# Routing scratch moved from a PSUM bank to SBUF, first group's ranks half a chunk later

## The chip, the cores and the metric

The kernel runs on one core of one Trainium2 chip. The metric is device time in microseconds (us) of one execution. The core has a TensorE (PE, with its weight loads as PEld), a VectorE (DVE), a ScalarE (ACT), a GpSimd (POOL) and a SyncE (SP), which work through their own instruction lists in order and wait for each other by semaphores. Operands lie in SBUF or in PSUM, whose banks hold 128 x 512 float32 each and take the results of matmuls.

## What is computed

The reference chains three layers, all in float32:

```python
# linear attention with decay: batch 4, heads 8, 768 steps, head_dim 48
for t in range(S):
    state = alpha[:, :, t, :, None] * state + np.einsum('bhd,bhe->bhde', k[:, :, t], v[:, :, t])
    y[:, :, t] = np.einsum('bhd,bhde->bhe', q[:, :, t], state)
# mixture of 8 experts, 3072 tokens, width 384, hidden 1024
logits = x @ w_gate
noise_scale = np.log1p(np.exp(x @ w_noise))
noisy_logits = logits + noise_scale * noise
top2 = np.argpartition(-noisy_logits, 2, axis=1)[:, :2]
...
h = np.maximum(x[mask] @ w1[e], 0.0)
out[mask] += top2_w[mask, k, None] * (h @ w2[e])
# dense gated layer, hidden 1536
return (a * b @ w_out).astype(np.float32)
```

## The kernel before

**Attention.** 24 chunks `i` of 128 tokens (6 for each of 4 batch entries) pass through the loop at L756 to L783. For each chunk TensorE does, in this order: the transposes of the next chunk's keys (`t_unit`, L643), the transposes of the previous chunk's result (`gx_unit`, L724), the part of the result that comes from the carried state (`inter`, L667), the scores of the next chunk (`sc_unit`, L651), the part of the result from inside the chunk (`intra`, L675), the gate's matmuls for the previous chunk (`gm_unit`, L736) and the state's update (`u_unit`, L702). VectorE masks the scores (L656) and makes the running products of the decay for a chunk three ahead (`prep`: scans L621 and L625, L620, L624). GpSimd multiplies keys and queries by them (L623, L626, L629), and with ScalarE it prepares expert weights beside this (`w_tick`: L110 on ScalarE, L111 on GpSimd). The state goes over VectorE's L717 or L714, GpSimd's L718 and ScalarE's L691.

**Routing beside it.** Four times in a chunk the loop calls `tick()`, which advances every generator in the list `side` to its next `yield`. So the order of the work is written out by hand: a `yield` more moves what follows by a quarter of a chunk. `gm_unit` appends a `routing` at the end of each set of chunks in `SUBS = (0, 5, 10, 14, 19, 24)`. It runs `choose`, which finds the two experts of every token of a set: ScalarE lists the logits out of the gate's bank 6 (L258, L259), ScalarE and GpSimd work out the noise's scale (L262 to L280), VectorE adds it (L284), and two passes of L290, L293, L294, L297, L298 find the largest and, after L302 has masked it, the second largest. Behind the last set of a group (`GROUPS = (14, 10)`, so sets 0 to 2 and sets 3 and 4) follow `route` and `lists`. `route` counts the tokens of each expert by a scan (L330), four matmuls into bank 5 (L337 to L343) that give the ranks, twelve small VectorE operations (L349 to L370), two wide comparisons (L376), 14 small matmuls (L384) and the sums with `lacc` (L388, L390), from which come the indices of expert 0's gathers (L479). `lists` does the same for the other seven experts (L412 to L449).

**Where the scratch lies.** `scratch` gives the small tiles of `choose` and `route` columns of bank 5 from 136 on, by way of `place`, unless the set is the last one, which has tiles in SBUF named `s_...`. The factor of the first scan, `d0[0]`, lies in bank 5 as well. `spot` gives the results of the matmuls their columns: the early ones in bank 5 (0 for ranks, 128 for lists), the others in bank 6 (`UG`) or a free bank.

**Behind it.** Eight experts of up and down products, each as three matmuls (`prod3`, L801 to L803), then the dense layer (L1117 to L1122). Of the first `up_unit`s some are given banks 5 and 6 among others.

Of the kernel before, what the change touches and what calls it, by code (L numbers as in the profile page):

```python
# [7 lines left out]
F32 = mybir.dt.float32  # L8
# [15 lines left out]
E = 8  # L24
# [13 lines left out]
GROUPS = (14, 10)  # L38
SUBS = (0, 5, 10, 14, 19, 24)
LAG = 3  # L40
WL = (E - 1) * NJ
# [16 lines left out]
def moe_kernel(ctx: ExitStack, tc, qka, afirst, v, wgn, noise, w1, w2, w3, out):  # L58
# [4 lines left out]
    def tl(pool, shape, dt, tag, **kw):  # L63
        uid[0] += 1
        return pool.tile(shape, dt, tag=tag, name=f"{tag}_{uid[0]}", **kw)
# [4 lines left out]
    def bank(i):  # L70
        return tl(psum, [128, 512], F32, f"bank{i}")
# [80 lines left out]
    rt = tc.alloc_tile_pool(name="rt", bufs=1, side="right")  # L152
# [3 lines left out]
    def trbank():  # L156
        trn[0] += 1
        return bank(trn[0] % 2)
# [13 lines left out]
    oh = [tl(rt, [128, NT, E], F32, f"oh{k}") for k in range(2)]  # L172
    oas = [tl(rt, [128, E, n + 1], F32, f"oa{n}") for n in GROUPS]
    B5 = bank(5)
    c0 = [136]

    def place(shape, name=None, dt=F32):

        if name:
            return tl(rt, [128, *shape], dt, name)  # L180
        n = 1
        for x in shape:
            n *= x
        a = B5[:, c0[0]:c0[0] + n]
        c0[0] += n
        a = a if dt == F32 else a.bitcast(dt)
        return a if len(shape) == 1 else a.rearrange("p (a b) -> p a b", a=shape[0])

    d0 = [place((E, GROUPS[0] + 1)), place((E, GROUPS[1] + 1), "d0")]
    SMALL = {}  # L190

    def scratch(name, shape, late, dt=F32):
        if late:
            return tl(rt, [128, *shape], dt, "s_" + name)
        if name not in SMALL:
            SMALL[name] = place(shape, None, dt)
        return SMALL[name]

    def iota(t, pattern, base=0, channel=0):
        nc.gpsimd.iota(t, pattern=pattern, base=base, channel_multiplier=channel,  # L200
# [18 lines left out]
    groups, i0 = [], 0  # L219
# [9 lines left out]
    def spot(kind, n, early=False):  # L229

        if early:
            return B5[:, (0, 128)[kind]:(0, 128)[kind] + n]
        c = (NP * 48, 288)[kind]
        return small[0][:, c:c + n] if small else trbank()[:, :n]

    def choose(s):
# [10 lines left out]
        def scr(name, *shape):  # L247
            return scratch(name, (5, *shape), last)[:, :n]
# [62 lines left out]
    def route(g):  # L311

        tiles = groups[g]
        n = len(tiles)
        i0 = tiles[0]
        sh = [128, n, E]
        last = g == len(groups) - 1
# [5 lines left out]
        def scr(name, dt=F32):  # L323
            return scratch(name, (n,), last, dt)
# [5 lines left out]
        nc.vector.tensor_tensor_scan(xc.rearrange("p e j -> p (e j)"), d0[g].rearrange("p e j -> p (e j)"),  # L330
                                     oa.rearrange("p e j -> p (e j)"), 0.0, op0=ALU.mult, op1=ALU.add)
        carry[0] = xc[:, :, n]
        for _ in range(LAG - 1):
            yield
        pb = spot(0, n * E + E + 1, not last)
        pc = pb[:, n * E:n * E + E]
        nc.tensor.matmul(pc, ones, xc[:, :, n], start=True, stop=True)  # L337
# [42 lines left out]
        for _ in range(LAG - 1):  # L380
            yield
        pl = spot(1, NJ, not last)
        for j in range(n):
            nc.tensor.matmul(pl, ats[j // m][:, j % m], bt[:, j], start=j == 0, stop=j == n - 1)  # L384
# [21 lines left out]
    def lists(g):  # L406

        i0, i1 = groups[g][0], groups[g][-1] + 1
        n = i1 - i0
        pi, ki, pf, kf = (tl(rt, [128, max(GROUPS), 2], dt, x)[:, :n]  # L410
                          for x, dt in (("ei", I32), ("ri", I32), ("rf", F32), ("e1", F32)))
        nc.vector.tensor_scalar(pi, slot[:, i0:i1], 127, None, op0=ALU.bitwise_and)  # L412
        nc.vector.tensor_scalar(ki, slot[:, i0:i1], 7, None, op0=ALU.logical_shift_right)
        nc.vector.tensor_copy(pf, pi)
        nc.vector.tensor_copy(kf, ki)
        sets = [(a, b) for a, b in zip(SUBS, SUBS[1:]) if i0 <= a < i1]
        hot = {}

        def make(s):
            j0, j1 = s  # L420
            m = j1 - j0
            at, eq, bt = (tl(rt, [128, HOT, 2, w_], F16, x, bufs=2)[:, :m]
                          for x, w_ in (("at", 128), ("eqk", WL), ("bt", WL)))
            for out_, src, val in ((at, lane, pf), (eq, keys[:, NJ:], kf)):
                w_ = src.shape[-1]
                nc.vector.tensor_tensor(out_.rearrange("p a k w -> p (a k) w"),
                                        src[:, None, :].to_broadcast([128, 2 * m, w_]),
                                        val[:, j0 - i0:j1 - i0].rearrange("p a k -> p (a k)")[:, :, None]
                                        .to_broadcast([128, 2 * m, w_]), op=ALU.is_equal)
                yield  # L430
            for k in range(2):
                nc.vector.tensor_tensor(bt[:, :, k], eq[:, :, k],
                                        token[:, j0:j1, None].to_broadcast([128, m, WL]), op=ALU.mult)
            hot[s] = m, at, bt

        yield from make(sets[0])
        for s, after in zip(sets, sets[1:] + [None]):
            if after:
                yield from make(after)
            else:  # L440
                for _ in range(LAG - 1):
                    yield
            m, at, bt = hot.pop(s)
            pl = spot(1, WL)
            for j in range(m):
                for k in range(2):
                    nc.tensor.matmul(pl, at[:, j, k], bt[:, j, k], start=j + k == 0, stop=j == m - 1 and k == 1)
            yield
            nc.vector.tensor_tensor((idx if s[1] == NT else lacc)[:, NJ:], pl, lacc[:, NJ:], op=ALU.add)  # L449
        yield  # L450
# [99 lines left out]
    def routing(s):  # L550
        yield from choose(s)
        g = group_of[SUBS[s]][0]
        if SUBS[s + 1] == groups[g][-1] + 1:
            yield from route(g)
            yield from lists(g)
        if SUBS[s + 1] == NT:
            for q in range(NJ):
                gather(1, q)
                yield
            yield from weights()  # L560
# [521 lines left out]
    for f in range(NF1):  # L1082
# [5 lines left out]
        if f in (4, 5, 7):  # L1088
            i = min(f - 4, 2)
# [69 lines left out]
    for u in range(NB * NF2):  # L1159
        blk, f = divmod(u, NF2)  # L1160
# [127 lines left out]
```

## Time and profile before

| what | us |
|---|---|
| median of 3 runs (1049.27 to 1050.80) | 1050.78 |
| the profiled execution, its own time | 1048.68 |
| its span in the trace | 1046.9 |
| TensorE busy | 1004.8 (96%) |
| VectorE busy | 563.0 (54%) |
| GpSimd busy | 411.9 (39%) |
| ScalarE busy | 384.9 (37%) |

The span runs from the first to the last recorded instruction; 1.8 us of the execution lie outside it. A row of a timeline gives the start, the duration, the engine, the line of the kernel, the operation, the tiles written and read, and, in brackets, how long the engine was idle before it and whose work ended that. `bank` stands for a PSUM tile, every other name for an SBUF tile or DRAM. Shares of busy time are averages over stages: attention with the routing takes the first 150 us, and from then on TensorE is busy almost without a gap.

### The profile page before, as it was taken

Reading aid. Unit: us, or ns where it says so; the run is one execution under the profiler, and the core shown is the slowest. Engines: PE = TensorE matmul, PEld = TensorE weight load, DVE = VectorE, ACT = ScalarE, POOL = GpSimd, SP = SyncE. Lnnn points to the kernel's source line nnn. Section 1 sums busy time; section 2 is a strip of 40 time slices with the busy share of each in tenths; the row PEclk is TensorE's granted clock in tenths of the full one; section 3 lists DMA queues with packets and bytes.
Section 4 is the critical chain, followed back from the end, with each engine's and each line's share of the span. In section 5 each row is a group of like instructions: output and inputs, shape, how many; then the busy total and the mean of one; then the engine's idle time right before and its main releaser. Section 6 shows DMA issues by size and latency. Waiting matters only on the chain.

```text
span 1046.9 us, 17559 instructions
## 1 busy us (share of the span) xinstructions
PE 1004.8 (96%) x6686; PEld 929.2 (89%) x6686; DVE 563.0 (54%) x987; ACT 384.9 (37%) x831; POOL 411.9 (39%) x443
## 2 busy tenths in 40 slices
PE   7998789999999999999999799999999999999996
PEld 5887679999999999999989688888888888888886
DVE  8999667576767776777646354242233232333221
ACT  2555331454454454545434243222222222222221
POOL 5688432575667686868644244020020020000000
PEclk9999779999999999999999899999999999999999
DMA  8787111669686869687845635131040140020000
GB/s 327 262 300 266 34 54 38 184 182 257 181 235 199 228 204 267 208 226 239 214 138 161 168 99 144 52 91 31 32 115 6 46 106 1 31 61 1 31 1 33
DMA packets 121491, 142.71 MB, mean 136 GB/s; under 512 B 68400, under 2 KB 105392, under 8 KB 121392
## 3 DMA queue, kind: packets, MB, share of 16 engines
q1 hardware_dynamic: 114864, 121.71, 38.7%
q0 software_dynamic: 6528, 19.67, 6.6%
q8 instruction: 64, 1.05, 0.4%
q14 instruction: 35, 0.29, 0.1%
HBM read 102.21 MB, written 39.12 MB: 135 GB/s over the span
## 4 chain that ended last, share of the span: by engine, by line
PE 86%; DVE 7%; DMA 2%; POOL 2%; issue 2%; ACT 1%; SPq 0%; POOLq 0%; ACTq 0%; DVEq 0%
PE bank L801 26%; PE bank L802 26%; PE bank L803 26%; PE bank L651 2%; PE bank L667 1%; DVE pm L656 1%; DVE D L621 1%; DVE A L625 1%; PE bank L675 1%; PE bank L643 1%; PE bank L702 1%; PE bank L611 1%; DMA wd<-w 0%; DMA raw<-xt 0%; PE bank L487 0%
## 5 line engine op out<-in xcount | busy, mean ns | idle before, releaser
L1119 DVE TENSOR_TENSOR p<-bank,a 128x512 f32<-128x512 f32 x72 | 49.8, 691 | 253.5 <-PE bank L803 253.5
L111 POOL TENSOR_TENSOR W<-wst,W 128x384 fp32r<-128x384 f32 x136 | 146.1, 1085 | 91.0 <-ACT W L110 83.1
L801 PE MATMUL bank<-X,W 128*128 128x416 f32 (+4 forms) x474 | 168.7, 356 | 2.9 <-DVE HB L846 2.5
L801 PE MATMUL bank<-HB,W 128*128 128x416 f32 (+4 forms) x474 | 167.2, 353 | 0.9 <-DVE o L874 0.9
L802 PE MATMUL bank<-X,W 128*128 128x416 f32 (+3 forms) x474 | 167.9, 354 | 0.0
L803 PE MATMUL bank<-X,W 128*128 128x416 f32 (+3 forms) x474 | 167.7, 354 | 0.0
L803 PE MATMUL bank<-HB,W 128*128 128x416 f32 (+3 forms) x474 | 166.5, 351 | 0.0
L802 PE MATMUL bank<-HB,W 128*128 128x416 f32 (+3 forms) x474 | 166.5, 351 | 0.0
L975 POOL DMA_INDIRECT row<-y,row x48 | 47.1, 981 | 203.9 <-DVE row L983 170.4
L1117 ACT ACTIVATE a<-bank 128x512 f32<-128x512 f32 x72 | 43.0, 597 | 167.0 <-PE bank L803 167.0
L845 ACT ACTIVATE HB<-bank 128x416 fp32r<-128x416 f32 (+2 forms) x128 | 65.7, 516 | 105.2 <-PE bank L803 105.1
L1121 ACT ACTIVATE HB<-p 128x512 fp32r<-128x512 f32 x72 | 45.5, 632 | 157.1 <-DVE p L1119 157.1
L801 PEld LDWEIGHTS bank<-X,W 128*128 128x128 f32 x474 | 89.8, 189 | 7.4 <-DVE HB L846 3.2
L846 DVE SCALAR_TENSOR_TENSOR HB<-bank,HB 128x416 fp32r<-128x416 f32 (+2 forms) x128 | 72.7, 582 | 41.0 <-ACT HB L845 40.9
L801 PEld LDWEIGHTS bank<-HB,W 128*128 128x128 f32 x474 | 89.1, 188 | 4.9 <-DVE o L874 1.2
L803 PEld LDWEIGHTS bank<-X,W 128*128 128x128 f32 x474 | 89.7, 189 | 4.1
L802 PEld LDWEIGHTS bank<-X,W 128*128 128x128 f32 x474 | 89.7, 189 | 3.6
L803 PEld LDWEIGHTS bank<-HB,W 128*128 128x128 f32 x474 | 89.0, 188 | 4.0
L802 PEld LDWEIGHTS bank<-HB,W 128*128 128x128 f32 x474 | 89.0, 188 | 3.7
L1122 DVE TENSOR_TENSOR HB<-p,HB 128x512 fp32r<-128x512 f32 x72 | 49.8, 692 | 50.2 <-ACT HB L1121 50.2
L110 ACT ACTIVATE W<-wst 128x384 fp32r<-128x384 f32 x144 | 72.1, 515 | 8.8 <-DMA wst<-w 7.2
L479 POOL DMA_INDIRECT row<-xd,idx x56 | 58.6, 1046 | 39.9 <-DVE idx L388 23.2
(240 smaller groups left out, 1954.3 us busy)
## 6 DMA issues: line engine op xcount, KB each, us to landing
wst<-w SPq DMA_DIRECT2D x128, 192.0 KB, 4.3
ring<-qka SPq DMA_DIRECT2D x22, 768.0 KB, 6.5
wd<-w SPq DMA_DIRECT2D x36, 384.0 KB, 4.5
xt<-tb SPq DMA_DIRECT2D x12, 768.0 KB, 4.6
raw<-xt SPq DMA_DIRECT2D x48, 192.0 KB, 4.4
y<-o SPq DMA_DIRECT2D x56, 156.0 KB, 2.8
w3f<-u SPq DMA_DIRECT2D x36, 192.0 KB, 2.8
wst<-w3f SPq DMA_DIRECT2D x36, 192.0 KB, 3.0
```

Of the source, the lines that this page charges most:

```text
L110: nc.scalar.activation(h, raw, AF.Copy)
L111: eng.tensor_tensor(l, raw, h.bitcast(F32), op=ALU.subtract)
L479: nc.gpsimd.indirect_dma_start(out=t[:m], out_offset=None, in_=xd[:SPLIT * 128] if a else xd, in_offset=bass.IndirectOffsetOnAxis(ap=ix, a ...
L801: nc.tensor.matmul(ps[:, :m], ah, bh[:, :m], start=first, stop=False)
L802: nc.tensor.matmul(ps[:, :n], ah, bl[:, :n], start=False, stop=False)
L803: nc.tensor.matmul(ps[:, :n], al, bh[:, :n], start=False, stop=last)
L845: nc.scalar.activation(Hh[:, f, s], pu[:, :n], AF.Relu)
L846: nc.vector.scalar_tensor_tensor(Hl[:, f, s], pu[:, :n], 0.0, Hh[:, f, s].bitcast(F32), op0=ALU.max, op1=ALU.subtract)
L975: nc.gpsimd.indirect_dma_start(out=t, out_offset=None, in_=src, in_offset=bass.IndirectOffsetOnAxis(ap=row[:, i, k:k + 1], axis=0))
L1119: nc.vector.tensor_tensor(p, ps[1], a, op=ALU.mult)
L1121: nc.scalar.activation(h, p, AF.Copy)
L1122: nc.vector.tensor_tensor(l, p, h.bitcast(F32), op=ALU.subtract)
```

## The change

Three things change. The small tiles of `choose` and `route` and the factor of the first scan are SBUF tiles for all sets, named `s_...0` for the earlier sets and `s_...1` for the last. The early results of matmuls get columns 0 and 256 of bank 5, and the sums of the first group's `lists` are early too, so they go to bank 5 instead of bank 6. The first group's rank matmuls stand `LAG + 1` = 4 ticks behind the scan instead of `LAG - 1` = 2, half a chunk.

```diff
     B5 = bank(5)
-    c0 = [136]
-
-    def place(shape, name=None, dt=F32):
...
-    d0 = [place((E, GROUPS[0] + 1)), place((E, GROUPS[1] + 1), "d0")]
-    SMALL = {}
+    d0 = [tl(rt, [128, E, n + 1], F32, f"d0{i}") for i, n in enumerate(GROUPS)]
 
     def scratch(name, shape, late, dt=F32):
-        if late:
-            return tl(rt, [128, *shape], dt, "s_" + name)
-        if name not in SMALL:
-            SMALL[name] = place(shape, None, dt)
-        return SMALL[name]
+        return tl(rt, [128, *shape], dt, f"s_{name}{int(late)}")
...
         if early:
-            return B5[:, (0, 128)[kind]:(0, 128)[kind] + n]
+            return B5[:, 256 * kind:256 * kind + n]
...
         carry[0] = xc[:, :, n]
-        for _ in range(LAG - 1):
+        for _ in range(LAG - 1 if last else LAG + 1):
             yield
...
         n = i1 - i0
+        waiting = g == len(groups) - 1
...
-            pl = spot(1, WL)
+            pl = spot(1, WL, not waiting)
```

The changed file is 18 or 19 lines shorter ahead of the attention loop, so L667 there is L649, L702 is L684, L337 is L318 and L293 is L274.

On TensorE the ranks of the first group stood between the transposes of chunk 19 and its `inter`. `xc` is the scan's result and `bank_30` is bank 5. Before:

```order
L702 MATMUL bank_32_121<-v_1335,kn_1799 48x48 x8
L643 MATMUL bank_371_1877<-ident_71,ring_37_132 128x128 x4
L724 MATMUL bank_373_1884<-ident_71,x_1849 128x128 x3
L337 MATMUL bank_30_119<-xc_367_1859,ones_77 128x8
L340 MATMUL bank_30_119<-xc_367_1859,ones_77 128x1
L342 MATMUL bank_30_119<-oa_28_117,before_75 128x112
L343 MATMUL bank_30_119<-xc_367_1859,ones_77 128x112
L667 MATMUL bank_375_1894<-Sbd_45_151,ring_36_131 128x96 x4
```

Now they stand behind the gate's matmuls and ahead of the state's update (L684):

```order
L657 MATMUL bank_391_1906<-v_1344,pm_379_1838 64x48 x2
L718 MATMUL bank_33_122<-wgn_104,gx_1904 64x16 x6
L318 MATMUL bank_30_119<-xc_383_1875,ones_77 128x8
L321 MATMUL bank_30_119<-xc_383_1875,ones_77 128x1
L323 MATMUL bank_30_119<-oa_28_117,before_75 128x112
L324 MATMUL bank_30_119<-xc_383_1875,ones_77 128x112
L684 MATMUL bank_33_122<-v_1543,kn_1898 48x48 x8
```

So the chunk's own `inter`, scores and `intra` no longer have the scan ahead of them.

On VectorE one pass of `choose` (the second one of a set) stays where it is, behind the scan L625 and around the L717, and changes its operands. `r_m` and `r_mk` are SBUF tiles in both. Before:

```order
L625 SCALAR_TENSOR_TENSOR A_1371<-ring_38_133,bank_33_128 128x512
L302 SCALAR_TENSOR_TENSOR bank_30_119<-oh_26_115,bank_30_119 128x40
L290 TENSOR_REDUCE r_m_281_1381<-bank_30_119 128x5
L293 TENSOR_TENSOR bank_30_119<-bank_30_119,r_m_281_1381 128x40
L294 TENSOR_TENSOR bank_30_119<-bank_30_119,prio_107 128x40
L717 TENSOR_TENSOR ss_1421<-bank_32_121,sc_1324 128x192
L297 TENSOR_REDUCE r_mk_282_1382<-bank_30_119 128x5
L298 TENSOR_TENSOR oh_27_116<-bank_30_119,r_mk_282_1382 128x40
```

Now:

```order
L607 SCALAR_TENSOR_TENSOR A_1380<-ring_40_135,bank_34_129 128x512
L283 SCALAR_TENSOR_TENSOR s_nl_290_1389<-oh_26_115,s_nl_271_1319 128x40
L271 TENSOR_REDUCE r_m_292_1392<-s_nl_290_1389 128x5
L274 TENSOR_TENSOR s_eq_291_1391<-s_nl_290_1389,r_m_292_1392 128x40
L275 TENSOR_TENSOR s_eq_291_1391<-s_eq_291_1391,prio_107 128x40
L699 TENSOR_TENSOR ss_1432<-bank_33_122,sc_1333 128x192
L278 TENSOR_REDUCE r_mk_293_1393<-s_eq_291_1391 128x5
L279 TENSOR_TENSOR oh_27_116<-s_eq_291_1391,r_mk_293_1393 128x40
```

The order is the same; the operations that had one SBUF input and one in the bank have two in SBUF.

Further on VectorE the two wide comparisons L376, which stood directly behind the small route operations and one L717, now stand behind the next chunk's masks and `prep` (L602 to L607):

```order
L351 TENSOR_TENSOR bt_2025<-eqk_2024,s_val_414_1992 128x98
L638 TENSOR_TENSOR pm_427_2046<-bank_425_2036,causal_73 128x512
L638 TENSOR_TENSOR pm_428_2048<-bank_426_2037,causal_73 128x512
L602 MEMSET bank_34_129 128x3
L603 SCALAR_TENSOR_TENSOR D_44_147<-ring_41_136,bank_34_129 128x511
L606 RECIPROCAL bank_34_129<-D_44_147 128x4
L607 SCALAR_TENSOR_TENSOR A_2050<-ring_41_136,bank_34_129 128x512
L357 TENSOR_TENSOR at_2059<-lane_109,s_pf_412_1990 128x896
L357 TENSOR_TENSOR at_2089<-lane_109,s_pf_412_1990 128x896
```

They moved with the ranks, by half a chunk; the 14 matmuls that read `at` (L384 before) moved on TensorE to a place between a chunk's scores and its `intra`.

## Rows read from the trace of the kernel before

**Rows 1.** The page, part 4: shares of the chain by engine and line.

```profile
PE 86%; DVE 7%; DMA 2%; POOL 2%; issue 2%; ACT 1%; SPq 0%; POOLq 0%; ACTq 0%; DVEq 0%
PE bank L801 26%; PE bank L802 26%; PE bank L803 26%; PE bank L651 2%; PE bank L667 1%; DVE pm L656 1%; DVE D L621 1%; DVE A L625 1%; PE bank L675 1%; PE bank L643 1%; PE bank L702 1%; PE bank L611 1%; DMA wd<-w 0%; DMA raw<-xt 0%; PE bank L487 0%
```

**Rows 2.** The chain, 50 to 112 us: start, duration, engine, tile, line.

```profile
63.89 1.29 DVE pm L656 x2
...
77.09 0.11 DVE bank L284
...
83.99 0.56 DVE pm L656
...
94.41 0.69 DVE pm L656
...
108.55 0.31 DVE xc L330
```

**Rows 3.** The timeline, 100 to 126 us, TensorE and VectorE.

```profile
108.90 0.39 PE L337 MATMUL bank<-xc,ones 128*128 128x8 f32 x2 [2.76 <-DVE xc L330]
...
113.27 1.29 DVE L656 TENSOR_TENSOR pm<-bank,causal 128x512 f32<-128x512 f32 x2 [4.17 <-PE bank L651]
...
119.47 0.26 DVE L370 TENSOR_TENSOR bt<-eqk,bank 128x98 f16<-128x98 f16 x1
...
120.00 0.88 PE L702 MATMUL bank<-v,kn 128*48 128x48 f32 x16 [4.30 <-ACT bank L259]
...
121.03 0.36 DVE L717 TENSOR_TENSOR ss<-bank,sc 128x192 f32<-128x192 f32 x1 [1.30 <-PE bank L702]
...
125.64 0.69 DVE L656 TENSOR_TENSOR pm<-bank,causal 128x512 f32<-128x512 f32 x1 [2.27 <-PE bank L651]
```

**Rows 4.** Busy time by window (us, PE, PEld, DVE, ACT, POOL), granted clock.

```profile
112.00:114.00 2.00, 2.00 (x28) 1.77 (x28) 0.73 (x2) 0.00 (x0) 0.00 (x0) 0.50 0.03 8
```

**Rows 5.** The timeline, 147 to 161 us, TensorE.

```profile
158.03 0.33 PE L801 MATMUL bank<-X,W 128*128 128x384 f32 x1
```

**Rows 6.** Instructions of line L942 (ns min/median/max), and timelines around 105, 143 and 252 us.

```profile
L942 DVE TENSOR_SCALAR u<-wd x36: 339/348/1470, 194.1 to 532.7; 128x384 int32<-128x384 int32 x36
...
105.60 0.26 POOL L306 TENSOR_TENSOR oa<-oh,oh 128x32 f32<-128x32 f32 x1
...
143.47 0.66 DVE L426 TENSOR_TENSOR eqk<-keys,e 128x490 f16<-128x490 f16 x1
...
143.63 0.63 POOL L306 TENSOR_TENSOR oa<-oh,oh 128x40 f32<-128x40 f32 x1 [3.39 <-DVE oh L298]
...
144.05 0.23 DVE L307 TENSOR_TENSOR dm<-r_m,r_m 128x5 f32<-128x5 f32 x1
...
251.10 2.62 POOL L111 TENSOR_TENSOR W<-wst,W 128x384 fp32r<-128x384 f32 x2
...
252.76 1.17 DVE L942 TENSOR_SCALAR u<-wd 128x384 int32<-128x384 int32 x1
```

**Rows 7.** The timeline, 74 to 106 us, VectorE and GpSimd.

```profile
76.84 1.28 POOL L623 TENSOR_TENSOR ring<-ring,D 128x512 f32<-128x512 f32 x1
...
77.01 0.18 DVE L284 TENSOR_TENSOR bank<-r_sp,bank 128x40 f32<-128x40 f32 x1
...
78.08 1.27 POOL L626 TENSOR_TENSOR ring<-ring,A 128x512 f32<-128x512 f32 x1
...
79.46 0.51 POOL L718 TENSOR_TENSOR sc<-ss,aend 128x192 f32<-128x192 f32 x1
...
82.42 0.18 DVE L302 SCALAR_TENSOR_TENSOR bank<-oh,bank 128x40 f32<-128x40 f32 x1
...
82.65 1.27 POOL L626 TENSOR_TENSOR ring<-ring,A 128x512 f32<-128x512 f32 x1 [0.22 <-DVE bank L302]
...
82.87 0.21 DVE L293 TENSOR_TENSOR bank<-bank,r_m 128x40 f32<-128x40 f32 x1
```

**Rows 8.** Instructions of line L293: ns min/median/max, first and last start.

```profile
L293 DVE TENSOR_TENSOR bank<-bank,r_m x8: 198/199/208, 53.3 to 140.9; 128x40 f32<-128x40 f32 x6, 128x32 f32<-128x32 f32 x2
L293 DVE TENSOR_TENSOR s_eq<-s_nl,r_m x2: 200/200/201, 156.0 to 157.4; 128x40 f32<-128x40 f32 x2
```

More of the change, by code (lines that the diff above doesn't have):

```diff
@@ L174, in moe_kernel @@
     B5 = bank(5)
-    c0 = [136]
-    def place(shape, name=None, dt=F32):
[L179 to L187, printed above, removed]
-    d0 = [place((E, GROUPS[0] + 1)), place((E, GROUPS[1] + 1), "d0")]
-    SMALL = {}
-    def scratch(name, shape, late, dt=F32):
-        if late:
-            return tl(rt, [128, *shape], dt, "s_" + name)
-        if name not in SMALL:
-            SMALL[name] = place(shape, None, dt)
-        return SMALL[name]
+    d0 = [tl(rt, [128, E, n + 1], F32, f"d0{i}") for i, n in enumerate(GROUPS)]
+    def scratch(name, shape, late, dt=F32):
+        return tl(rt, [128, *shape], dt, f"s_{name}{int(late)}")
     def iota(t, pattern, base=0, channel=0):
```

## The prediction, made before the changed kernel ran

> **What bounds the kernel now.** I read the chain of waits first. Over the whole span it is TensorE by 86% [rows 1], and 78% of the span are the three products L801 to L803, which the change leaves as they are. So only the time ahead of them, attention with the routing beside it, can change, and what matters there is when these products may begin.
>
> Inside that stretch I read the chain again, with a window [rows 2]. TensorE is not the chain everywhere. VectorE carries it at 63.9 us, from before 77.09 to 83.99 and from 94.41 to 108.86. Those stretches hold the small VectorE operations of the second and third `choose`: L284, L290, L293, L294, L297, L298, then L302 and once more L290 to L298. The step at 83.99 us is the L656 that stands behind the whole pass. So a VectorE operation that gets longer there moves the end one for one.
>
> Then the timeline around the first group's ranks [rows 3]. L337 waits 2.76 us for the scan L330 and holds the whole of chunk 19's TensorE work behind it, since TensorE works in order. 11 us later L702 waits 4.30 us for ScalarE's L259, which lists the logits into bank 5 and had to wait for L370, the last of the twelve small route operations that use bank 5. VectorE pays too: its L656 stands idle for 4.17 us, its L717 for 1.30 us and the next L656 for 2.27 us, each time for TensorE. [...]
>
> **Part one, the ranks half a chunk later and the bank freed: a gain.** The four rank matmuls move behind chunk 19's scores, intra and gate matmuls. L330 is done at 108.86 us [rows 2] and they come after that, so the 2.76 us go. With the scratch in SBUF, L259 no longer has to wait for L370, so the 4.30 us go as well. What is late next is VectorE: without the idle time it is busy from there to the lists of the first group, and it holds the bound. Its end moves by the idle time it had for TensorE, 4.17 + 1.30 + 2.27 = 7.74 us. I take 0.7 us off for a new wait: the 14 matmuls L384 now stand one unit earlier on TensorE, behind two L376 on VectorE that stand a prep later. That makes **-7 us**. Bounds: 0, if the wait only changes its name, and -10, if the tail of the lists does not bind. In between lies the place where the lists' sums bind: the last of them shares bank 5 with the expert product that starts at 158.03 us [rows 5], which therefore waits for the sum.
>
> **Part two, the scratch in SBUF: a loss.** Each operation of `choose` reads and writes bank 5 now. Then it would read two SBUF tiles, and GpSimd is reading SBUF at the same time. What the trace says of such a pair [rows 6]: the scalar operation L942 takes 348 ns in the median. The one at 252.76 us stood beside GpSimd's L111 until 253.72 and took 1.17 us, ending 0.21 us behind it. Smaller ones do the same at 143.47 us: VectorE's L426, two SBUF inputs, ran until 144.13, and GpSimd's L306 took 0.63 us instead of the 0.26 of 105.60 us and ended at 144.26. VectorE's L307, 128x5 with two SBUF inputs, then took 0.23 us and ended at 144.28. So whoever comes second stands until the other is done, whatever its size. The bank forms stand beside GpSimd untouched: L284 at 77.01 us inside L623, and L293 at 82.87 us inside L626, both took about 0.2 us [rows 7].
>
> Now the price of one `choose`, with these rows. First pass: L284 would come at 77.01 us, while L623 runs until 78.12: +1.1 us. L293 then meets L626, which has started meanwhile (1.27 us long): +0.6 us. L294 and L298 meet the short GpSimd steps behind it, L718 (0.51 us) among them: +0.5 us. That is +2.2 us. Second pass: L302 comes as L623 is done and gets through. L626 starts 0.23 us behind it, so L293 stands for most of its 1.27 us: +1.0 us. L294, L298 and L307 meet L718 and an L111 (1.3 us each in rows 6): +1.0 us. That is +2.0 us, so 4.2 us for one `choose` with 8 to 9 such operations. The second and third `choose` lie on the chain and count in full, 8 us (the third has no L718 in its second pass, hence a little less than twice 4.2). The first hands its delay on to the L656 at 63.89 us; I count 2 us of its 4. Together **+10 us**. Bounds: 0, if these small operations slip in between, as the bank forms do, and +13, if all three count in full.
>
> The twelve route operations, now behind one more L717, and the two L376 become SBUF readers as well. They meet one L626 or L623 (1.27 us) and an L718 (0.51 us) [rows 7]: **+2 us**, rounded up; between 0 and, for a second meeting of that kind, 4. The fourth `choose` stands beside gathers for the most part and I count nothing for it; at worst it costs one more pass, 2 us, which the range holds.
>
> I count nothing for the reductions L290 and L297, though no row shows one with an SBUF input in the middle of a GpSimd operation. If all four of a `choose` stood for 0.42 us like the rest, the sum would be 5 us higher.
>
> [...]
>
> [...] The late `choose` already has its scratch in SBUF, at a time without GpSimd: its L293 take 200 ns, those in the bank 199 [rows 8]. So moving it saves nothing by itself. [...]
>
> The lists' sums in bank 5, and the other columns in it, move no operation of a length that counts; what waits for that bank is in the -7 us.
>
> **The sum.** 10 + 2 - 7 = +5 us against the profiled execution's 1048.68 us: 1053.7 us. That execution lies 2.1 us under the median of the three runs, 1050.78, so on their scale it is **1055.8 us**. A difference of 0.2%, 2.1 us, is about the least that a measurement tells from none.
>
> **Rivals.**
> - *Faster: the stall goes and the pair of engines does not collide.* 24 operations, 8 in each of three `choose`, carry the loss. If they wait less than 0.13 us each in the mean, where I count 0.42, that is 3 us, with the route's 2 us it is 5, and the gain of 7 wins by the 2.1 us that a measurement sees. With no loss at all the time is 1050.8 - 7 = 1043.8 us. For it: both engines leave gaps, and a VectorE operation of 0.2 us needs a small one. Against it: GpSimd's L623 and L626 stand back to back beside the first pass [rows 7], and rows 6 show no mercy for small ones. Chance 0.25.
> - *No change: both are real and about cancel*, within 2.1 us of 1050.8. It needs a loss of 5 to 9 us in all. Chance 0.12.
> - *Slower still: the clock.* TensorE would now wait 2 us at a pass, and behind a 2.76 us wait the clock fell to 0.50 [rows 3, 4]. In such a window TensorE does in 2 us what takes 1 at full clock. If TensorE is the bound there once in each of the three `choose`, 3 us come on top: 1059 us. Against it: in the second and third VectorE is the bound, and hides it. Chance 0.06.
> - *The change does not do what it says*: the wait at L702 stays, since L702 needs ScalarE, which has other work queued. Then only the loss is left, 1050.8 + 12 = 1063 us. L259 is free of L370 in the new order, so I give it no chance of its own; it is the upper end of the range.
>
> **How the numbers follow.** The forecast, a loss larger than the gain by more than 2.1 us, has 0.57, with its own range from 1053 to 1063 us. With the clock it makes slower 0.63; no change has 0.12, faster 0.25. The range goes from 1044 us, the stall gone with next to no loss, to 1063 us, the whole loss and no gain.
>
> **What would show it.** In the profile after: the L293 and L294 of the first three `choose` last 0.4 us and more in the mean, with ends that lie just behind those of L623, L626 or L111; the wait of L702 for L259 of 4.30 us is gone; the second and third `choose` end 6 to 8 us later than now, and the product of 158.03 us comes some 5 us later. I am wrong if these operations still take 0.20 us: then the loss is not there and the time is near 1044 us. The gain is wrong if the new L384 waits as long as L702 did.

## The result, and the profile after

The changed kernel takes 1058.31 us in the median of 5 runs (1055.67 to 1061.38), the kernel before 1050.78 (1049.27 to 1052.34). The ratio is 1.0077, with a 95% interval from 1.0052 to 1.0101: slower, by 7.5 us. The profiled execution took 1055.67 us, 7.0 more than the one before.

Where the time went shows when one follows the same matmuls through both traces. The gate's matmuls (L736, after the change L718) come once in a chunk; a row here is one of them, or one of the expert products (L801, now L783).

| place | before, us | after, us | later by |
|---|---|---|---|
| ahead of the first `choose` | 54.85 | 54.49 | -0.4 |
| behind the first | 64.31 | 68.99 | 4.7 |
| behind the second | 90.02 | 99.02 | 9.0 |
| in the third, last pass | 104.31 | 116.17 | 11.9 |
| behind the ranks' old place | 114.91 | 122.45 | 7.5 |
| behind the old wait of L702 | 126.50 | 128.60 | 2.1 |
| behind the comparisons (L376, now L357) | 131.51 | 138.28 | 6.8 |
| first expert product | 150.09 | 153.14 | 3.1 |
| tenth L801, in bank 5 | 158.03 | 164.59 | 6.6 |
| twentieth L801 | 164.76 | 172.18 | 7.4 |

From there on the distance hardly moves: up to the end of the trace it stays between 7.0 and 8.9 us.

The three `choose` lose 12.2 us, from -0.4 to 11.9. The timeline of the changed kernel over the first one, with the three engines that matter (the lines answer to [rows 7]):

```profile
52.49 1.27 POOL L605 TENSOR_TENSOR ring<-ring,D 128x512 f32<-128x512 f32 x1
52.66 1.16 DVE L265 TENSOR_TENSOR s_nl<-r_sp,s_lg 128x40 f32<-128x40 f32 x1
...
53.72 1.29 POOL L608 TENSOR_TENSOR ring<-ring,A 128x512 f32<-128x512 f32 x1
53.85 0.20 DVE L271 TENSOR_REDUCE r_m<-s_nl 128x5 f32<-128x40 f32 x1
...
60.77 1.26 POOL L608 TENSOR_TENSOR ring<-ring,A 128x512 f32<-128x512 f32 x1 [0.21 <-DVE s_nl L283]
60.98 1.11 DVE L274 TENSOR_TENSOR s_eq<-s_nl,r_m 128x40 f32<-128x40 f32 x1
...
62.24 0.35 DVE L699 TENSOR_TENSOR ss<-bank,sc 128x192 f32<-128x192 f32 x1
...
62.74 0.73 PE L718 MATMUL bank<-wgn,gx 128*64 128x16 f32 x12 [2.63 <-DVE r_mk L278]
63.13 1.00 POOL L111 TENSOR_TENSOR W<-wst,W 128x384 fp32r<-128x384 f32 x1
63.16 1.00 DVE L288 TENSOR_TENSOR dm<-r_m,r_m 128x5 f32<-128x5 f32 x1
```

L265 works on 40 columns and takes 1.16 us; it ends at 53.82, 0.06 us behind GpSimd's L605. L274 ends at 62.09, 0.06 us behind L608. L288 works on five columns and takes 1.00 us beside L111, whose end lies 0.03 us ahead of its own. I call this the lock: in these three rows the operation that comes second lasts until the other is done, 0.03 to 0.06 us beyond its end. The same lines grouped, in ns min/median/max (the first of [rows 8] had 198/199/208 for what is now L274):

```profile
L265 DVE TENSOR_TENSOR s_nl<-r_sp,s_lg x5: 201/903/1169, 52.7 to 159.5; 128x40 f32<-128x40 f32 x4, 128x32 f32<-128x32 f32 x1
L274 DVE TENSOR_TENSOR s_eq<-s_nl,r_m x10: 190/824/1116, 54.2 to 161.8; 128x40 f32<-128x40 f32 x8, 128x32 f32<-128x32 f32 x2
L279 DVE TENSOR_TENSOR oh<-s_eq,r_mk x10: 199/503/694, 55.9 to 162.5; 128x40 f32<-128x40 f32 x8, 128x32 f32<-128x32 f32 x2
```

Taken one by one against 0.15 to 0.21 us before, the operations of `choose` last 4.5 us longer in the first, 4.5 in the second and 3.2 in the third. That makes 12.2 us, as much as TensorE's gate matmuls are late by then.

None of this is a wait in the profile's sense: the lock lies inside the duration and counts as busy time (VectorE 579.2 us, before 563.0). TensorE's waits are where it shows (the view of waits, 0 to 170 us: in total, times, longest):

```profile
PE bank L718 <- DVE r_mk L278: 7.9, 3, 2.6
PE bank L365 <- DVE at L357: 3.6, 2, 1.8
...
PE bank L684 <- ACT s_lg L240: 1.5, 2, 1.1
...
PE bank L783 <- DVE lacc L431: 0.9, 1, 0.9
```

L718 writes bank 6, which VectorE's L699 reads just ahead of L278. In the second pass L699 stands behind L274, so three times TensorE waits about 2.6 us for a sum of 0.35 us. Behind each of the three waits the granted clock falls to 0.50, as it did behind the old stall [rows 4]; of the 850 slices of 0.2 us up to 170 us it is at 1.00 in 724, at 0.50 in 114 and between the two in 12. Busy time by window (us, PE, PEld, DVE, ACT, POOL, granted clock, DMA share, GB/s), behind the first, behind the second and around the third:

```profile
64.00:66.00 2.00, 2.00 (x14) 1.91 (x11) 1.96 (x5) 1.16 (x3) 0.37 (x2) 0.50 0.98 371
...
94.00:96.00 2.00, 2.00 (x12) 2.00 (x11) 1.89 (x5) 1.44 (x4) 0.43 (x1) 0.50 0.04 8
...
114.00:116.00 2.00, 0.00 (x0) 0.00 (x0) 1.90 (x7) 0.09 (x1) 1.78 (x3) 1.00 0.26 93
116.00:118.00 2.00, 1.83 (x35) 1.80 (x36) 1.95 (x7) 1.45 (x4) 0.87 (x2) 0.88 0.00 0
118.00:120.00 2.00, 2.00 (x12) 1.83 (x10) 1.90 (x3) 0.89 (x2) 0.62 (x1) 0.50 0.00 0
```

The old stall itself is gone, and with it 9.8 us between the third `choose` and 128.60 us. The lines that answer to [rows 3], and what came 10 us later:

```profile
122.45 0.49 PE L718 MATMUL bank<-wgn,gx 128*64 128x16 f32 x12
...
122.87 0.39 PE L318 MATMUL bank<-xc,ones 128*128 128x8 f32 x2
...
124.26 0.56 PE L684 MATMUL bank<-v,kn 128*48 128x48 f32 x16
...
133.07 3.14 DVE L357 TENSOR_TENSOR at<-lane,s_pf 128x896 f16<-128x896 f16 x2
...
134.19 0.33 PE L365 MATMUL bank<-bt,at 128*128 128x7 f16 x7 [1.84 <-DVE at L357]
...
135.22 1.05 POOL L611 TENSOR_TENSOR aend<-af,D 128x4 f32<-128x4 f32 x1
...
136.26 0.35 PE L365 MATMUL bank<-bt,at 128*128 128x7 f16 x7 [1.74 <-DVE at L357]
136.54 1.95 PE L657 MATMUL bank<-v,pm 128*64 128x48 f32 x32
```

L318 follows L718 without a wait, and neither row of L318 or L684 shows one. But L357 is blocked in its turn: two comparisons take 3.14 us, 2.08 before, and GpSimd's L611, 0.21 us in the median, takes 1.05 beside them. TensorE waits 3.6 us for them and goes on at half clock (L657 1.95 us, 1.14 at 121.48 us), as the window shows: 4.7 us lost in that chunk.

```profile
136.00:138.00 2.00, 1.74 (x35) 1.72 (x37) 1.80 (x6) 0.00 (x0) 1.56 (x6) 0.50 0.00 0
```

Of the small route operations, too, some are blocked. The longest is L331, which reads one SBUF tile only; in the bank, as L350, it took 0.18 us:

```profile
125.81 1.27 POOL L608 TENSOR_TENSOR ring<-ring,A 128x512 f32<-128x512 f32 x1 [0.21 <-PE bank L706]
...
126.03 1.08 DVE L331 TENSOR_SCALAR s_pi<-s_val 128x14 int32<-128x14 int32 x1
```

At the end of the routing there is one thing more, the product that shares bank 5 with the lists' sums (it answers to [rows 5]):

```profile
163.31 0.37 PE L429 MATMUL bank<-bt,at 128*128 128x49 f16 x8 [1.81 <-DVE lacc L431]
164.59 0.44 PE L783 MATMUL bank<-X,W 128*128 128x384 f32 x1 [0.91 <-DVE lacc L431]
```

### The profile page after: what moved, and what is told of

It reads as the page before. It is cut to its first block, busy times and chain, and to the rows that moved or that the text cites. A ratio compares the mean times of both kernels' runs of the same rounds, so it can differ in the third digit from the quotient of the medians.

```text
span 1053.9 us, 17559 instructions
## 1 busy us (share of the span) xinstructions
PE 1008.5 (96%) x6686; PEld 932.1 (88%) x6686; DVE 579.2 (55%) x987; ACT 385.0 (37%) x831; POOL 414.1 (39%) x443
## 3 DMA queue, kind: packets, MB, share of 16 engines
q8 instruction: 64, 1.05, 0.4%
## 4 chain that ended last, share of the span: by engine, by line
PE 83%; DVE 6%; DMA 2%; issue 1%; POOL 1%; ACT 1%; SPq 0%; DVEq 0%; ACTq 0%; POOLq 0%
PE bank L783 26%; PE bank L784 26%; PE bank L785 26%; PE bank L649 1%; PE bank L657 1%; DVE D L603 1%; PE bank L633 1%; DVE pm L638 1%; POOL row L957 1%; DVE A L607 1%; DMA wd<-w 1%; DMA raw<-xt 0%; PE bank L625 0%; PE bank L469 0%; DMA y<-o 0%
## 5 line engine op out<-in xcount | busy, mean ns | idle before, releaser
L111 POOL TENSOR_TENSOR W<-wst,W 128x384 fp32r<-128x384 f32 x136 | 146.8, 1090 | 92.6 <-ACT W L110 81.6
L783 PE MATMUL bank<-X,W 128*128 128x416 f32 (+4 forms) x474 | 168.8, 356 | 4.2 <-DVE HB L828 2.8
L783 PE MATMUL bank<-HB,W 128*128 128x416 f32 (+4 forms) x474 | 167.2, 353 | 0.8 <-DVE o L856 0.8
L783 PEld LDWEIGHTS bank<-X,W 128*128 128x128 f32 x474 | 89.9, 190 | 8.7 <-DVE HB L828 3.5
L783 PEld LDWEIGHTS bank<-HB,W 128*128 128x128 f32 x474 | 89.1, 188 | 4.9 <-DVE o L856 1.2
L110 ACT ACTIVATE W<-wst 128x384 fp32r<-128x384 f32 x144 | 72.1, 515 | 10.4 <-DMA wst<-w 8.4
```

Of the source, the lines that this page charges most:

```text
L110: nc.scalar.activation(h, raw, AF.Copy)
L111: eng.tensor_tensor(l, raw, h.bitcast(F32), op=ALU.subtract)
L783: nc.tensor.matmul(ps[:, :m], ah, bh[:, :m], start=first, stop=False)
```

## The experiments

Three theories were on the table. Theory 1: VectorE's operations with two SBUF inputs stand beside GpSimd. Theory 2: the loss is in the lists' sums in bank 5, which expert products wait for. Theory 3: it is TensorE's half clock behind new waits. Each kernel was timed against the kernel before on the same chip; that one had 1049.2 to 1049.4 us in the median there. The medians of the variants come from 6 to 12 runs each, which in most of them lie 5 to 13 us apart, so a difference of 1 or 2 us between two of them is not clear of the spread.

**The scratch alone.** The kernel before with the change's `d0` and `scratch`, nothing else.

```diff
...
-        if late:
-            return tl(rt, [128, *shape], dt, "s_" + name)
-        if name not in SMALL:
-            SMALL[name] = place(shape, None, dt)
-        return SMALL[name]
+        return tl(rt, [128, *shape], dt, f"s_{name}{int(late)}")
```

> The kernel before with one part of the change: the scratch and the scan's factor in SBUF; ranks and lists' sums stay. Theory 1 (VectorE's operations with two SBUF inputs stand beside GpSimd): the three early choose lose 10 to 13 us, L259 no longer waits for L370, which gives some 4 back, the wait of 2.76 us for the scan stays: 1055 to 1061 us, L293 and L284 at 0.8 us and more in the median. Theory 2 (the loss is the first lists' sums in bank 5, which the expert products wait for, and not the scratch): 1046 to 1051 us, those operations at 0.2 us. Theory 3 (the loss is TensorE's half clock behind new waits): 1051 to 1054 us, and only as far as TensorE, not VectorE, is busy in the slow stretches.

Measured: 1061.13 us, ratio 1.0116 [1.0090, 1.0142]: 11.8 us slower, just over the upper end of theory 1. L274 (L293 before) has a median of 819 ns. L265 (L284 before) has one of 199 ns, against what I expected, but up to 1154. TensorE's waits:

```profile
PE bank L717 <- DVE r_mk L278: 7.3, 3, 2.6
...
PE bank L683 <- ACT s_lg L240: 2.5, 3, 1.1
...
PE bank L318 <- DVE xc L311: 1.7, 1, 1.7
```

The sums of the lists are in bank 6 here and the loss is larger than in the whole change, so theory 2 does not carry it. The old wait of 4.30 us for L259 (here L240) is gone without any delay of the ranks; the longest one left is 1.1 us. The wait for the scan is 1.7 us instead of 2.76.

**The delay alone.**

```diff
-        for _ in range(LAG - 1):
+        for _ in range(LAG - 1 if last else LAG + 1):
```

> The kernel before with one part: the first group's ranks half a chunk later. Theories 1 and 2: the waits of 2.76 us at L337 and 4.30 us at L702 go, 1042 to 1046 us. If the delay alone only moves the wait, because the scratch still shares bank 5 with the logits' copy L259: 1049 to 1053 us.

Measured: 1040.36 us, ratio 0.9918 [0.9897, 0.9939]: 9.0 us faster than before and 18 faster than the changed kernel; that is below the 1042 to 1046 us of theory 1. The timeline of TensorE:

```profile
109.39 0.39 PE L337 MATMUL bank<-xc,ones 128*128 128x8 f32 x2
...
111.42 0.56 PE L702 MATMUL bank<-v,kn 128*48 128x48 f32 x16 [0.57 <-ACT bank L259]
...
121.46 0.49 PE L384 MATMUL bank<-bt,at 128*128 128x7 f16 x14 [1.95 <-DVE at L376]
```

L702 comes at 111.42 instead of 120.00 us, with a wait of 0.57. L259 still writes bank 5, but the small route operations now come behind it in the program, so the scratch in the bank is no obstacle. In the trace the first expert product comes 10.7 us earlier than before (139.36 against 150.09 us). Behind the lists, for which later products wait, 7.1 us of this are left (157.71 against 164.76 us for the twentieth L801), from there on between 6.3 and 7.5, and 7.4 at the last.

**The lists' sums back in bank 6**, everything else as changed.

```diff
-        waiting = g == len(groups) - 1
...
-            pl = spot(1, WL, not waiting)
+            pl = spot(1, WL)
```

> The changed kernel with the first group's lists' sums back in bank 6. Theory 1: the choose keep their loss, only the wait of the expert product in bank 5 for the last sum (0.9 us, and 1.8 us of the sums' matmuls behind each other) may go: 1055 to 1058 us. Theory 2: the loss goes with them, 1043 to 1047 us.

Measured: 1058.08 us, ratio 1.0096 [1.0063, 1.0130]. The wait of the product in bank 5 goes, and the time stays, 0.2 us from the changed kernel's 1058.31. Theory 2 falls. This kernel is the delay with the scratch in SBUF, so beside the one above it gives the price of the scratch: 1058.08 - 1040.36 = 17.7 us, between 13 and 24 by the intervals of the two ratios. The profiled executions of the two, 1053.72 and 1040.44 us, lie 13.3 us apart.

**The scratch back in bank 5**, delay and lists' sums as changed (the sums in the columns that the ranks have left).

```diff
...
+        if late:
+            return tl(rt, [128, *shape], dt, "s_" + name)
+        if name not in SMALL:
+            SMALL[name] = place(shape, None, dt)
+        return SMALL[name]
...
-            return B5[:, 256 * kind:256 * kind + n]
+            c = 128 if kind and n == NJ else 0
+            return B5[:, c:c + n]
```

> The changed kernel with the scratch and the scan's factor back in bank 5 (the lists' sums stay in bank 5 too, in the columns that the ranks have left). Theory 1: the choose lose nothing, L293 at 0.2 us, the stall is gone, 1043 to 1049 us. Theory 2: as slow as the changed kernel, 1055 to 1059 us.

Measured: 1041.78 us, ratio 0.9927 [0.9907, 0.9948]. That is a little less than theory 1 expected and far from theory 2. Between this kernel and the delay alone lie the lists' sums in bank 5: 1.4 us (1041.78 against 1040.36), and the ranges of the two overlap.

**Only the scratch of `choose` in SBUF**, with the delay.

```diff
...
-        if late:
+        if late or name in ("lg", "nl", "eq", "nl2"):
...
```

> The kernel with the delay alone, and of the scratch only the four tiles of choose (lg, nl, eq, nl2) in SBUF. Theory 1: the operations of choose carry most of the loss, 10 to 13 us over the 1040.4 of the delay alone: 1050 to 1054 us. If route's tiles or the scan's factor carry it: 1040 to 1044 us.

Measured: 1055.61 us, ratio 1.0057 [1.0039, 1.0075]: 15.3 us over the delay alone, more than expected. The profiled executions, 1052.98 and 1040.44 us, lie 12.5 us apart.

**Only the scratch of `route`** and the scan's factor, with the delay.

```diff
...
-        if late:
+        if late or name in ("pi", "ki", "pf", "kf", "val"):
...
```

> The kernel with the delay alone, and of the scratch only route's tiles (pi, ki, pf, kf, val) and the scan's factor in SBUF. Theory 1: the two wide comparisons and some of the small operations stand beside GpSimd, 2 to 5 us over 1040.4: 1042 to 1046 us. If they carry most of the loss: 1050 us and more.

Measured: 1043.12 us, ratio 0.9922 [0.9898, 0.9945]: 2.8 us over the delay alone by the medians, but the ranges of the runs and the intervals of the ratios (0.9922 and 0.9918) overlap. TensorE now waits 3.5 us for the comparisons (1.95 with the delay alone). 15.3 and 2.8 make 18.1, against the 17.7 of both together, so the two parts add up as far as the spread lets one see.

```profile
PE bank L384 <- DVE at L376: 3.5, 2, 1.8
```

**GpSimd's work cut, with the scratch in the bank and in SBUF.** This tells the lock from anything that an SBUF operand costs by itself. The edit is the same in both.

```diff
...
+            w_ = 512 if i == 0 else 64
...
-            e.tensor_tensor(t[:, :512], t[:, :512], At, op=ALU.mult)
+            e.tensor_tensor(t[:, :w_], t[:, :w_], At[:, :w_], op=ALU.mult)
...
-            w_split()
+            w_split(None)
```

> The kernel with the delay alone, GpSimd's two multiplications in the attention loop cut to 64 of 512 columns from the second chunk on, and the weights' low parts of that loop written by ScalarE as a plain copy, so that GpSimd has little to do. It leaves out 7/8 of the products with the decay and the true low parts. It is the other half of the pair with e8: alone it says nothing but how much GpSimd's length costs, 1030 to 1041 us.

> The changed kernel with the lists' sums in bank 6, with the same cut of GpSimd's work as e7 (the same part is left out). Without the cut this pair lies 17.7 us apart (1058.1 and 1040.4). Theory 1: with nothing to stand beside, the operations of choose take 0.2 us and the pair lies 0 to 4 us apart. If the SBUF forms cost by themselves, or the columns' place does, it still lies 12 us and more apart.

Measured: 1043.76 us, ratio 0.9933 [0.9910, 0.9956], and 1044.76 us, ratio 0.9959 [0.9939, 0.9978]. The pair that lay 17.7 us apart lies 1.0 us apart, within the spread of the runs. The first is above 1041, against what I expected. ScalarE has more to do in both, which may be the reason; no run tests it. The same operations in the second kernel:

```profile
L268 DVE TENSOR_TENSOR s_nl<-r_sp,s_lg x5: 166/174/202, 51.3 to 143.8; 128x40 f32<-128x40 f32 x4, 128x32 f32<-128x32 f32 x1
L277 DVE TENSOR_TENSOR s_eq<-s_nl,r_m x10: 189/191/202, 51.9 to 146.1; 128x40 f32<-128x40 f32 x8, 128x32 f32<-128x32 f32 x2
L278 DVE TENSOR_TENSOR s_eq<-s_eq,prio x10: 191/199/499, 52.2 to 146.3; 128x40 f32<-128x40 f32 x8, 128x32 f32<-128x32 f32 x2
```

174 and 191 ns, from SBUF to SBUF, where the changed kernel had 903 and 824. The one L278 with 499 ns, at 75.89 us, stands beside the state's product on GpSimd, which the cut leaves as it was (75.83 us, 0.51 us long). So the loss is the meeting of the two engines; that is shown.

**The state's update one tick earlier**, with the scratch in SBUF and in the bank.

```diff
-            tick()
             if i + 1 < NT:
                 u_unit(i + 1)
                 s_unit(i + 1)
+            tick()
             tick()
```

> The changed kernel with the lists' sums in bank 6 (1058.1 us), and the state's update issued one tick earlier in each chunk, so that VectorE's sum of the state stands ahead of the choose operation that waits longest, not behind it. In the changed kernel the gate's matmuls wait 7.9 us for that sum in three places. If the loss reaches TensorE by way of this one wait: it falls to 3 us or less, 1050 to 1054 us. If VectorE's whole list is late and the wait is only where that shows: the wait moves to another place and the time stays at 1055 to 1059 us.

> The same step on the kernel with the delay alone (1040.4 us): nothing of choose stands there for long, so 1039 to 1042 us by either reading; it shows what the step does by itself.

Measured: 1057.00 us, ratio 1.0072 [1.0050, 1.0093], and 1046.63 us, ratio 0.9970 [0.9955, 0.9985]. The second expectation failed: the step by itself costs 6.3 us. TensorE waits 5.1 us for `gx` there and 3.3 for the comparisons, against 0.6 and 2.0 with the delay alone. In the first kernel the 7.9 us for L278 are gone, and in their place the gate's matmuls wait as follows:

```profile
PE bank L717 <- ACT gx L707: 6.9, 4, 3.2
...
PE bank L717 <- DVE ss L698: 3.4, 3, 1.2
```

So the wait moved and the time hardly did, 1.1 us, which speaks for VectorE's whole list being late. But the step is no clean test, since it costs something of its own: against its own partner in the bank the SBUF form loses 10.4 us, not 17.7. How much of the loss runs through L699 alone stays open.

**Other lengths of the delay**, on the kernel with the delay alone: `LAG` and `LAG + 2` instead of `LAG + 1`.

> The kernel with the delay alone, 3 ticks instead of 4. If the scan must only be done when the ranks come: 1040 to 1043 us. If the ranks still meet the scan behind the chunk's first matmuls: 1043 to 1049 us.

> The kernel with the delay alone, 5 ticks instead of 4. If the delay only has to be long enough: 1039 to 1042 us. If the lists' end already binds: 1042 to 1046 us.

Measured: 1046.53 us with 3 ticks, ratio 0.9971 [0.9958, 0.9985], and 1042.13 us with 5, ratio 0.9930 [0.9908, 0.9953]. With 3 the ranks come too early by 0.80 us, and L702 behind them waits:

```profile
108.42 0.39 PE L337 MATMUL bank<-xc,ones 128*128 128x8 f32 x2 [0.80 <-DVE xc L330]
...
114.46 0.88 PE L702 MATMUL bank<-v,kn 128*48 128x48 f32 x16 [2.41 <-ACT bank L259]
```

With 5 the range of the runs overlaps that of 4, and the time lies between the two expectations, so it decides neither. Four ticks and the scratch in the bank has the lowest median of the versions that ran, 1040.36 us.

## Why the prediction was right, point by point

The direction was right, and the time, 1058.31 us against 1055.8 forecast, lies in the range and in the forecast's own range.

- **The lock between the engines** is the mechanism, as forecast, and it was readable from three small rows of the trace before [rows 6]. L293 and L294 were to last 0.4 us and more in the mean. In the first three `choose` they (now L274 and L275) have 0.66, but L274 makes it alone: 0.99, and L275 0.33. One `choose` was priced at 4.2 us; by the durations it cost 4.5, 4.5 and 3.2. The loss was mis-sized: +10 us for the three, measured 12.2 in the trace up to the third one. The step that failed in it is "I count 2 us of its 4" for the first `choose`: it handed on 5.0, all of it. The second gave 4.3, as counted, the third 2.9. So the second and the third end 9.0 and 11.9 us later, not 6 to 8.
- **By kernels the loss is larger than in the traces.** With the route's 2 us it was to be 12; the medians give 17.7 for the scratch and 15.3 for `choose` alone. This does not lie behind the third `choose`: against the delay alone, the trace of the kernel with only `choose` in SBUF is 11.7 us late in the third one's last pass (115.74 against 104.00 us) and 11.5 at the last gate matmuls (149.17 against 137.63). Its profiled execution is one of its faster ones, in a range from 1051.12 to 1059.28 us. What makes other executions longer no trace shows.
- **The route's tiles**, +2 us, between 0 and 4: 2.8 by the medians, not clear of the spread. In the trace of the changed kernel four lines last longer than before, by 2.6 us together (L331, L334, L348 and the two L357).
- **The gain**, -7 us: the delay alone gives 9.0 us, with an interval from 6.4 to 10.8 by its ratio, and 6.3 to 7.5 us at the expert products of its trace. The term stands. Inside it the new wait at L384, 0.7 us forecast, came to 1.95; in the changed kernel, where the lock lengthens L357, it came to 3.6, not much less than the 4.30 that were to be the sign of a wrong gain.
- **What belongs to which part.** The prediction put the end of L702's wait down to both parts together. It takes only one: the scratch alone ends it, and so does the delay. So the delay is worth 9.0 us with the scratch in the bank, but only 3.1 with it in SBUF (1061.13 to 1058.08, and the ranges of these two overlap). Reading the -7 as a gain of the whole change was right; as a gain over the scratch alone it would have been wrong.
- **The rival of the clock** came true in part: behind each of the three waits the clock is at 0.50. Most of it is hidden, as the prediction had it, since VectorE is the bound: its longer durations make up the 12.2 us by themselves. Behind the slow stretches it waits for TensorE twice, 1.00 us behind the second `choose` (0.92 before) and 0.32 behind the third:

```profile
98.16 1.29 DVE L638 TENSOR_TENSOR pm<-bank,causal 128x512 f32<-128x512 f32 x2 [1.00 <-PE bank L633]
...
121.58 1.29 DVE L638 TENSOR_TENSOR pm<-bank,causal 128x512 f32<-128x512 f32 x2 [0.32 <-PE bank L633]
```

So a full clock could have given back about 1.3 us there, an estimate from these two waits, and theory 3 is not the main loss. What the half clock behind L357 adds to the 4.7 us of that chunk no run divides; L657 lasts 1.7 times as long there (1.95 us against 1.14), not the twice that the prediction reckoned with. That the time, 1058.31, comes close to the 1059 of this rival is chance.
- **The reductions**, priced at nothing by the author's choice, with no row of before to show it, were not lengthened. In the changed kernel none of the 20 takes longer than 198 ns, though they stand among operations that take five times their usual time, and the one at 53.85 us stands inside GpSimd's L608:

```profile
L271 DVE TENSOR_REDUCE r_m<-s_nl x10: 186/196/197, 53.8 to 161.5; 128x5 f32<-128x40 f32 x8, 128x4 f32<-128x32 f32 x2
L278 DVE TENSOR_REDUCE r_mk<-s_eq x10: 174/196/198, 55.7 to 162.2; 128x5 f32<-128x40 f32 x8, 128x4 f32<-128x32 f32 x2
```

- **The price of a bank operand.** With GpSimd's work cut, L265 and L274 (L268 and L277 there) take 174 and 191 ns in SBUF. In the bank, with the delay alone, they took 182 and 198:

```profile
L284 DVE TENSOR_TENSOR bank<-r_sp,bank x4: 174/182/203, 52.4 to 124.8; 128x40 f32<-128x40 f32 x3, 128x32 f32<-128x32 f32 x1
...
L293 DVE TENSOR_TENSOR bank<-bank,r_m x8: 198/198/207, 53.0 to 131.5; 128x40 f32<-128x40 f32 x6, 128x32 f32<-128x32 f32 x2
```

That is 8 and 7 ns less in SBUF for each operation, so the forecast's 0 us for moving them was nearly right.
- **The lists' sums in bank 5**, priced at nothing of their own, make 0.2 and 1.4 us in the two pairs, neither clear of the spread.

## What to carry to other kernels

Here an operand's place also decided which engine its reader met: L293 took 199 ns in the bank, 824 in SBUF beside GpSimd (L274) and 191 in SBUF with GpSimd's work cut (L277). Before moving scratch from PSUM to SBUF, count the VectorE operations that will then read two SBUF tiles (and, as L331 shows, some that read one), and look at what GpSimd does in those microseconds. A change with two parts can hide a good one: here the delay gains 9 us and the scratch loses 18 by the medians, and only running each alone shows it. A wait that two edits can each remove must not be counted twice, nor given to one of them.

## What the runs showed that was not expected

A VectorE operation on five columns (L288) took 1.00 us, and GpSimd's L611 on four columns 1.05 us, beside an operation of the other engine on 384 and on 896 columns (L111 and L357); the profile shows both as busy, with no releaser. So the chain of waits goes astray there. In the changed kernel it steps from L288 to a DMA that has nothing to do with it (the chain, 54 to 66 us: start, duration, what):

```profile
60.67 2.50 DMA xd<-x
63.17 0.99 DVE dm L288
```

What gives such a meeting away is the duration against the same line elsewhere, and an end that lies just behind the other engine's (0.03 to 0.06 us in the rows of the changed kernel above). Which of the two is second the recorded starts do not always tell: in the trace before, VectorE's L952 starts at 220.84 us, 0.17 ahead of GpSimd's L111, lasts 1.62 us (0.50 at its shortest) and ends 0.43 behind it.
